# One fused attention and feed-forward kernel: its engine order planned anew, and the first batch's summary rows copied on chip without a transfer

## The chip, the cores and the metric

The kernel runs on one core of a Trainium2 chip. The metric is device time in microseconds (us), the median of three runs. One more execution was profiled; its trace is the source of all rows here.

## The reference

Four batches, eight heads, 768 positions, head size 64. Every query attends to a window of near keys and to 24 summary keys of its sequence; the result goes through a feed-forward block of 512 by 2048.

```python
k_sum = k.reshape(B, H, nb, 32, D).max(axis=3)     # 24 summary keys per head
v_sum = v.reshape(B, H, nb, 32, D).mean(axis=3)    # 24 summary rows of v
scores_l = scale * q @ k.T, kept where |i - j| < 16
scores_s = scale * q @ k_sum.T + log(32)
a = softmax(concat(scores_l, scores_s))
x = a @ concat(v, v_sum)
h = x @ w_in                                       # 3072 x 512 by 512 x 2048
out = (h * erf(softplus(h))) @ w_out
```

## The kernel before

The 3072 rows are worked in six chunks of 512; a chunk has four quads (a quad is one pair of heads in one chunk), so there are 24 quads, numbered in order. For a quad the names are: `scores` (TensorE: mask, near keys, summary keys), `softmax` (VectorE `red`: the row maxima, tile stats; ScalarE `exps`, tile prf; VectorE or ScalarE `norm`), `transp` (TensorE turns the weights, ScalarE copies them to tile ptr), `av` (TensorE: ptr times the value window vw, tile px), `xsplit` (ScalarE or VectorE `high`, VectorE `low`, tile x). The feed-forward block takes the chunks in passes of a quarter of w_in and w_out: `mm1` (tile h), `hout`, activations, `gsplit`, `mm2` (tile ops, lines L1009 and L1013). Float32 operands of the large products are split in a high and a low part, three matmuls for one. Weights arrive packed; `convert` unpacks one unit in three VectorE instructions on tile a, and `split` makes its high part on ScalarE (tile w) and its low part on VectorE.

The last 24 of the 120 rows of each value window of batch 0 are the summary rows. `vsum_first` makes them: six matmul steps on TensorE (tile vs), one copy of the result (tile vsum), and for each of the first four quads one spread of its 24 rows over the eight blocks of the window (tile vwf), which `av` of that quad needs. A spread can be an engine's copy or a transfer on SP's queue.

The order of work is not that of the program text. Every step is handed to a planner, `Plan`, with engines it may run on and a cost in us for each, and with what it reads and writes. `Plan.due` works out from the order of the text when a step would be due; `Plan.order` then goes through time, and at each moment an engine takes, of the steps ready, the one with the lowest key: due time (for TensorE the step's number) plus a correction from the table `TUNE`, which has a row for a step's number: correction, price of an activation table change, which table, and the engine if it is fixed. Every engine's instructions are issued in the planned order, so a step that waits holds up those behind it on its engine; the same goes for SP, which issues the loads. Where the planner sees TensorE idle in the first stage, it puts matmuls on zeros there (`busy`, L1050); seven more stand at the start.

The first steps are numbered: 0 to 7 the loads of keys and queries of quads 0 to 3 (kf, qf in turn), 8 and 9 the values (vt), 10 to 13 the value windows, 14 to 17 the first four weight units; 18 to 27 quad 0's summary keys, scores and softmax (27 its norm), 28 to 35 quad 1's (28 its summary keys, 35 its norm), 36 to 43 quad 2's (43 its norm); 44 to 49 the matmuls of the summary rows, 50 their copy, 51 to 54 the four spreads; 55 to 62 quad 3's (62 its norm); 63 to 72 two weight units; from 73 `transp`, `av`, `xsplit` of quads 0 to 3 with `mm1` between.

```python
key[n] = later + (n if "PE" in o["eng"] else o["due"])
if eng is not None:
    o["eng"] = {eng: o["eng"][eng]}
...
on({"ACT": 0.95, "SP": 0.45} if p else {"DVE": 1.13, "ACT": 0.95}, lambda e, p=p: rows_(e, p), [f"vsum0{p}", f"vwf{p}"], [f"vwg{p}"])
```

Of the kernel before, what the change touches and what calls it, by code (L numbers as in the profile page):

```python
# [58 lines left out]
class Plan:  # L59
# [44 lines left out]
    def order(self, free, window, tune, table):  # L104
# [14 lines left out]
        for o in ops:  # L119
            n = o["n"]  # L120
            later, change[n], which, eng = tune.get(n, (0.0, PEN, 0, None))
            key[n] = later + (n if "PE" in o["eng"] else o["due"])
            if eng is not None:
                o["eng"] = {eng: o["eng"][eng]}
                o["two"] = True
            if o["table"]:
                o["pick"] = o["table"][which]
# [64 lines left out]
def block_attention_mlp(ctx: ExitStack, tc: tile.TileContext, q_t, k_nat, k_win, v_tok, v_nat, v_win, w_in, w_out, out):  # L192
# [16 lines left out]
    def ps(name, tag):  # L209
        return psum.tile([128, 512], F32, name=name, tag=tag)  # L210
# [83 lines left out]
    def first_dma(us, fn, r=(), w=(), **kw):  # L294
        return P.add({"SP": us}, lambda e: fn(), r, w, hold=2.0, land=-1.0, **kw)
# [31 lines left out]
    def load_w(u):  # L327
        kind, g, r = u
        n = raw_slot(u)

        def go():
            rw = raws[u] = slot(n, [128, 2, 512, 2], U32, "rw")
            src = (w_in[2 * g + r] if kind == "i" else w_out[2 * g + r]).bitcast(U32).rearrange("p c (f t) -> p c f t", t=2)
            nc.sync.dma_start(out=rw, in_=src)
        if u in units[:4]:
            first_dma(2.6, go, w=[f"w{n}"])
        else:
            dma(1112, go, w=[f"w{n}"])
# [169 lines left out]
    def load_qk_first(p):  # L508
        st[p] = dict(qb=qfs[:, p], vw=vws[p // 2][:, p % 2])
        first_dma(2.7 if p == 1 else 0.97, lambda: nc.sync.dma_start(out=kfirst[p], in_=k_nat[0, p]), w=[f"kf{p}"])  # L510
        first_dma(0.66, lambda: nc.sync.dma_start(out=qfs[:, p], in_=q_t[0, p]), w=[f"qf{p}"])

    def load_v_first():
        for n in range(2):
            def go(n=n):
                for t in range(3):
                    nc.sync.dma_start(out=vts[n][:, t], in_=v_tok[3 * n + t])
            first_dma(2.1 + 0.15 * n, go, w=[f"vt{n}"])

    def load_vw_first(p):  # L520
        first_dma(1.35, lambda: nc.sync.dma_start(out=st[p]["vw"], in_=v_win[0, p]), w=[f"vwf{p}"])
# [4 lines left out]
    def vsum_first(bank):  # L526
        def go(t):
            if t == 0:
                tiles[bank] = ps("vs", bank)
            nc.tensor.matmul(tiles[bank][0:NK], lhsT=pick[:, 20 - 4 * t:140 - 4 * t], rhs=vts[t // 3][:, t % 3], start=(t == 0), stop=(t == 5))  # L530
        for t in range(6):
            pe(0.87, lambda t=t: go(t), [f"vt{t // 3}"], [bank])
        def summed():
            nc.scalar.copy(vsum[LW:NK], tiles[bank][LW:NK].rearrange("s (p c) -> s p c", p=NP))
        act(0.5, summed, [bank], [f"vsum0{p}" for p in range(NP)])
        def rows_(e, p):
            o, i = st[p]["vw"][LW:NK], vsum[LW:NK, p:p + 1, :].to_broadcast([NS, NB, 128])
            e.dma_start(out=o, in_=i) if e is nc.sync else copy(e, o, i)
        for p in range(NP):
            on({"ACT": 0.95, "SP": 0.45} if p else {"DVE": 1.13, "ACT": 0.95}, lambda e, p=p: rows_(e, p), [f"vsum0{p}", f"vwf{p}"], [f"vwg{p}"])  # L540
# [24 lines left out]
    def load_quad_v(qd):  # L565
        ch, p, seqs = where(qd)
        s = st[qd]

        def go():
            s["vw"] = sb([128, NB, 128], F32, "vw")  # L570
            nc.sync.dma_start(out=s["vw"], in_=v_win[ch, p])
        dma(585, go, w=["vw"])
        for b, js in seqs:
            n = js.stop - js.start
            dma(100 if n == NB else 50, lambda b=b, js=js, n=n: nc.sync.dma_start(out=s["vw"][LW:NK, js], in_=vsum_rows(b, p).to_broadcast([NS, n, 128])),
                [f"vsum{b % 2}{p}"], ["vw"])

    PA = ("pA", "pB")

    def scores(qd, banks=PA):  # L580

        s = st[qd]

        def mask():
            for n in banks:
                tiles[n] = ps(n, n)
            s["sc"] = [tiles[n] for n in banks]
            m0 = mask_at[qd // NP % 3]
            for sc in s["sc"] if qd < MQ else []:

                nc.tensor.matmul(sc[:, 0:NI * NK], lhsT=ident_h, rhs=mask_h[:, m0:m0 + NI], start=True, stop=False, skip_group_check=True)
                nc.tensor.matmul(sc[:, 0:NI * NK].rearrange("q (i c) -> q i c", i=NI)[:, :, LW:NK], lhsT=ones, rhs=cst.rearrange("o (i c) -> o i c", i=NI), start=False, stop=False, skip_group_check=True)

        def keys(parts):
            for j in range(NB):
                for a in range(2):
                    r, o = slice(64 * a, 64 * a + 64), slice(64 * (j % 2), 64 * (j % 2) + 64)
                    for n, rhs in parts(r, j):
                        n += j // 2 * NK
                        nc.tensor.matmul(s["sc"][a][o, n:n + rhs.shape[-1]], lhsT=s["qb"][r, 64 * j:64 * j + 64], rhs=rhs, start=qd >= MQ, stop=True, skip_group_check=True)  # L600

        def near(r, j):

            kn, k0 = kfirst[qd], 64 * j - 16
            return [(0, kn[r, k0:k0 + LW])] if j else [(16, kn[r, 0:LW - 16])]

        def both():
            mask()
            keys(lambda r, j: [(0, s["kw"][r, j])])
        if qd >= NP:  # L610
            pe(0.98 if qd >= MQ else 1.56, both, [f"qb{qd % 2}", f"kw{qd % 2}"] + (["mh"] if qd < MQ else []), banks, small=1)
        else:
            pe(0.58, mask, ["mh"], banks, small=1)
            pe(0.96, lambda: keys(near), [f"qf{qd}", f"kf{qd}"], banks, small=1)
            pe(0.5, lambda: keys(lambda r, j: [(LW, ksum[r, 0, qd])]), [f"qf{qd}", f"ksum0{qd}"], banks, small=1)
# [104 lines left out]
    def av(qd, bank):  # L720
# [3 lines left out]
        def go():  # L724
            xo = s["xo"] = ps("px", bank)
            for j in range(NB):
                o = slice(64 * j, 64 * j + 64)
                for a in range(2):
                    r = slice(64 * a, 64 * a + 64)
                    if qd < DT:  # L730
                        b = 64 * (NI * a + j // 2)
                        nc.tensor.matmul(xo[r, o], lhsT=s["vw"][0:NK, j, r], rhs=s["pt"][0:NK, j % 2, b:b + 64], start=True, stop=True)  # L732
                    else:
                        z = 2 * (j % 2)
                        nc.tensor.matmul(xo[r, o].rearrange("d (a q) -> d a q", a=2), lhsT=s["vw"][0:NK, j, r], rhs=s["pt"][0:NK, z:z + 2, NI * a + j // 2], start=True, stop=True)  # L735
# [572 lines left out]
```

## Time and profile before

| | before |
|---|---|
| median of 3 runs | 600.12 us (599.73 to 600.18) |
| the profiled execution | 599.8 us |
| its span, first to last instruction | 598.0 us, so 1.8 us lie around it |
| mean granted TensorE clock | 0.998 of full speed |
| last matmul ends, last copy ends | 594.05 us, 594.66 us into the span |

PE is TensorE's matmul, PEld its weight load, DVE VectorE, ACT ScalarE, SP the engine whose queue (SPq) issues the loads. A matmul's end in the trace is modelled, and matmuls overlap; the step from one start to the next is shorter than the duration shown.

### The profile page before, as it was taken

The numbers are of one execution on the slowest core, as the hardware profiler recorded it, in microseconds if no ns is written. First come the engines' busy times: TensorE is split into PE (matmuls) and PEld (weight loads), VectorE is DVE, ScalarE is ACT, GpSimd is POOL, SyncE is SP. The second block draws the span as 40 slices with busy tenths as digits, with TensorE's granted clock in tenths as the row PEclk, the third lists the DMA queues.
The fourth block names the chain that finished last, engine by engine and source line by source line (L and its number), as shares of the span: only waits on it lengthen the run. The fifth ranks groups of instructions, "written<-read, shape, count | busy, mean of one in ns | idle before, by whom it ended". The sixth has DMA issues, their size and how long they took to land.

```text
span 598.0 us, 11682 instructions
## 1 busy us (share of the span) xinstructions
PE 590.6 (99%) x4495; PEld 486.1 (81%) x4495; DVE 476.4 (80%) x1001; ACT 424.3 (71%) x824; POOL 4.0 (1%) x30
## 2 busy tenths in 40 slices
PE   8899999999999999999999999999999999999997
PEld 4675666878888889989888888888888888888885
DVE  5999999888999987866989769669778677556553
ACT  6989879989879794674885964846646654852570
POOL 2000000000000000000000000000000000000000
PEclk9999999999999999999999999999999999999999
DMA  8999777668997989899998888787897864774621
GB/s 330 358 418 344 282 253 284 221 247 316 318 344 245 345 323 338 290 351 370 313 376 315 323 310 323 267 302 269 292 304 263 309 226 146 252 243 178 237 72 70
DMA packets 47586, 169.93 MB, mean 284 GB/s; under 512 B 4460, under 2 KB 16940, under 8 KB 34988
## 3 DMA queue, kind: packets, MB, share of 16 engines
q1 hardware_dynamic: 47388, 169.07, 78.1%
q8 instruction: 35, 0.57, 0.4%
q14 instruction: 19, 0.16, 0.1%
q10 hardware_dynamic: 144, 0.13, 0.1%
HBM read 135.66 MB, written 31.46 MB: 279 GB/s over the span
## 4 chain that ended last, share of the span: by engine, by line
PE 96%; ACT 1%; DVE 1%; issue 0%
PE ops L1013 41%; PE h L839 15%; PE ha L891 12%; PE hb L885 7%; PE ops L1009 5%; PE hb L891 4%; PE hb L882 4%; PE pA L600 3%; PE px L735 3%; PE px L732 1%; DVE stats L639 1%; PE pA L687 1%; PE idle L1050 1%; ACT prf L647 0%; PE pB L600 0%; ACT ptr L692 0%
## 5 line engine op out<-in xcount | busy, mean ns | idle before, releaser
L1013 PE MATMUL ops<-w,gh 128*128 128x512 f32 x704 | 230.1, 393 | 0.0
L1013 PEld LDWEIGHTS ops<-w,gh 128*128 128x128 f32 x704 | 132.3, 188 | 27.8 <-issue 0.9
L1013 PE MATMUL ops<-w,gl 128*128 128x512 f32 x352 | 137.5, 391 | 0.0
L1264 ACT ACT_TABLE_LOAD x98 | 125.7, 1283 | 1.7
L839 PE MATMUL h<-x,w 128*128 128x512 f32 x384 | 97.0, 402 | 0.0
L298 ACT COPY hc<-hb 128x256 f32<-128x256 f32 x65 | 23.9, 373 | 102.9 <-PE hb L882 57.0
L839 PEld LDWEIGHTS h<-x,w 128*128 128x128 f32 x384 | 71.1, 188 | 18.5 <-issue 3.6
L1013 PEld LDWEIGHTS ops<-w,gl 128*128 128x128 f32 x352 | 66.2, 188 | 11.8
L989 DVE TENSOR_TENSOR hc<-wt,hc 128x1024 f32<-128x1024 f32 x44 | 53.0, 1219 | 10.7 <-ACT wt L977 10.7
L647 ACT ACTIVATE prx<-prx,stats 128x120 f32<-128x120 f32 x160 | 61.0, 384 | 0.2
L996 DVE TENSOR_TENSOR gl<-hc,gh 128x1024 fp32r<-128x1024 f32 x44 | 53.6, 1220 | 1.0 <-ACT gh L298 0.2
L930 DVE TENSOR_TENSOR hc<-hb,hc 128x256 f32<-128x256 f32 x96 | 38.7, 418 | 15.8 <-ACT hc L298 14.6
L977 ACT ACTIVATE wt<-wt 128x1024 f32<-128x1024 f32 x48 | 50.1, 1058 | 0.4
L965 ACT ACTIVATE wt<-hc 128x1024 f32<-128x1024 f32 x32 | 33.0, 1055 | 8.2 <-DVE hc L930 8.0
L298 DVE CAST gh<-hc 128x1024 fp32r<-128x1024 f32 x37 | 25.5, 690 | 10.6 <-PE ops L1013 9.5
L885 PE MATMUL hb<-w,ws 128*128 128x512 f32 x96 | 30.2, 396 | 0.0
L647 ACT ACTIVATION_READ_ACCUMULATOR prx<-prx,stats 128x1 f32 x160 | 30.0, 187 | 0.0
L1009 PE MATMUL ops<-a32s,gw 128*128 128x512 f32 x64 | 29.6, 597 | 0.0
L633 DVE CUSTOM_DVE_ANT_0 prx<-pA,mask_sb 128x120 f32<-128x120 f32 x64 | 14.2, 278 | 17.7 <-PE pB L600 17.4
L298 DVE COPY hc<-hb 128x256 f32<-128x256 f32 x31 | 13.0, 418 | 18.0 <-PE hb L882 13.8
L891 PE MATMUL ha<-w,ws 128*128 128x256 f32 x192 | 27.2, 283 | 0.0
L891 PE MATMUL ha<-x,w 128*128 128x256 f32 x192 | 27.1, 282 | 0.0
(172 smaller groups left out, 959.8 us busy)
## 6 DMA issues: line engine op xcount, KB each, us to landing
w<-dr SPq DMA_DIRECT2D x36, 1024.0 KB
ws<-ds SPq DMA_DIRECT2D x30, 1024.0 KB
vw<-v_win SPq DMA_DIRECT2D x20, 512.0 KB
kw<-k_win SPq DMA_DIRECT2D x20, 480.0 KB
rw<-w_in SPq DMA_DIRECT2D x8, 1024.0 KB
rw<-w_out SPq DMA_DIRECT2D x8, 1024.0 KB
dr<-w SPq DMA_DIRECT2D x8, 1024.0 KB
dt<-ot SPq DMA_DIRECT2D x16, 512.0 KB
```

The lines of the kernel that those rows point to most:

```text
L298: e.copy(o, i) if e is nc.scalar else e.tensor_copy(o, i)
L647: nc.scalar.activation(s["pr"][:, j], s["pr"][:, j] if qd >= MQ else s["sc"][j // NI][:, i * NK:(i + 1) * NK], AF.Exp, scale=-1.0 if qd >= ...
L839: nc.tensor.matmul(hs[k, f][:, 0:T], lhsT=w[m], rhs=xt[ch, cc][:, x], start=(cc == 0 and n == 0), stop=(cc == 3 and n == 2))
L885: nc.tensor.matmul(full, lhsT=w[0], rhs=y, start=first and c == 0, stop=c == 1, skip_group_check=True)
L891: nc.tensor.matmul(half, lhsT=w[m], rhs=y[:, l], start=first and c == 0 and i == 0, stop=c == 1 and i == 2, skip_group_check=True)
L930: on({"DVE": 0.43}, lambda e: e.tensor_tensor(hc[k, n][:, m, z], bank(n, "b")[:, R], hc[k, n][:, m, z], op=ALU.add), [pair_banks(n)[1]], [ ...
L977: act(0.96, lambda n=n: nc.scalar.activation(wt[k, n], wt[k, n], AF.Erf, scale=-1.0 if k < SOFT else 1.0), [s], [s], table=("sig",), after ...
L989: e.tensor_tensor(hc[k, n], wt.pop((k, n)), hc[k, n], op=ALU.mult)
L996: e.tensor_tensor(gs[k, n][1], hc.pop((k, n)), f32(gs[k, n][0]), op=ALU.subtract)
L1009: nc.tensor.matmul(os_[ch, t], lhsT=x[0][:, i % 2, t * 128:(t + 1) * 128], rhs=w32["o", g, i // 2][:, i % 2], start=first, stop=last)
L1013: nc.tensor.matmul(os_[ch, t], lhsT=x[y][:, i % 2, t * 128:(t + 1) * 128], rhs=w[m], start=first and n == 0, stop=last and n == 2)
L1264: nc.scalar.preload_act_table_set(sets[o["load"]])
```

## The change

Three things are edited. The correction table `TUNE` is replaced as a whole: 1303 rows for 1114, 8 of them as before, with numbers up to 2101 in both. The planner's costs of the first loads and of a few first-stage steps are set to other values, and the first eight loads get keys of their own that put them in the order 0, 1, 3, 2, 8, 4, 5, 9. The spread of the summary rows may run on ScalarE or VectorE only; the new table puts all four on ScalarE, where before three were there and quad 2's was a transfer on SP. The copy of the summary rows (50) may now be VectorE's too, and the table keeps it on ScalarE. `OWN` and `ASKED` are empty, so their branches issue nothing; the number of steps is the same. In the table the rows are shown broken over lines, those of the steps that the text speaks of.

```diff
-TUNE = {0: (-400.0, 1.5, 0, None), 1: (-300.0, 1.5, 0, None), 2: (-100.0, 1.5, 0, None), 3: (-200.0, 1.5, 0, None),
...
-27: (392.5856, 1.5, 0, None), 35: (42.72401, 1.5, 0, None), 43: (39.54326, 1.5, 0, None),
-51: (-22.99868, 1.5, 0, 'ACT'), 52: (-1.271128, 1.5, 0, 'ACT'), 53: (0, 1.5, 0, 'SP'), 54: (-212.8407, 1.5, 0, 'ACT'),
-62: (-0.1662937, 1.5, 0, 'ACT'),
...
+TUNE = {0: (-25.14396, 1.5, 0, None), 2: (0.2021052, 1.5, 0, None),
...
+27: (31.6296, 1.5, 0, None), 28: (-7.221647, 1.5, 0, None), 35: (3.818883, 1.5, 0, 'DVE'), 43: (13.99603, 1.5, 0, 'DVE'),
+50: (86.021, 1.5, 0, 'ACT'), 51: (50.85707, 1.5, 0, 'ACT'), 52: (23.98324, 1.5, 0, 'ACT'), 53: (0.01018608, 1.5, 0, 'ACT'), 54: (0.09698313, 1.5, 0, 'ACT'),
...
-            key[n] = later + (n if "PE" in o["eng"] else o["due"])
+            key[n] = later + (n if "PE" in o["eng"] else o.get("first", o["due"]))
-        return P.add({"SP": us}, lambda e: fn(), r, w, hold=2.0, land=-1.0, **kw)
+        return P.add({"SP": us}, lambda e: fn(), r, w, hold=2.0, land=-0.9, **kw)
-            first_dma(2.6, go, w=[f"w{n}"])
+            first_dma(2.5, go, w=[f"w{n}"])
-        first_dma(2.7 if p == 1 else 0.97, lambda: nc.sync.dma_start(out=kfirst[p], in_=k_nat[0, p]), w=[f"kf{p}"])
-        first_dma(0.66, lambda: nc.sync.dma_start(out=qfs[:, p], in_=q_t[0, p]), w=[f"qf{p}"])
+        first_dma((1.05, 1.0, 1.0, 1.0)[p], lambda: nc.sync.dma_start(out=kfirst[p], in_=k_nat[0, p]), w=[f"kf{p}"])
+        first_dma((0.65, 1.4, 0.65, 0.65)[p], lambda: nc.sync.dma_start(out=qfs[:, p], in_=q_t[0, p]), w=[f"qf{p}"])
-            first_dma(2.1 + 0.15 * n, go, w=[f"vt{n}"])
+            first_dma(2.0 + 0.85 * n, go, w=[f"vt{n}"])
-        first_dma(1.35, lambda: nc.sync.dma_start(out=st[p]["vw"], in_=v_win[0, p]), w=[f"vwf{p}"])
+        first_dma(1.28, lambda: nc.sync.dma_start(out=st[p]["vw"], in_=v_win[0, p]), w=[f"vwf{p}"])
-        act(0.5, summed, [bank], [f"vsum0{p}" for p in range(NP)])
+        on({"ACT": 0.55, "DVE": 0.6}, lambda e: copy(e, vsum[LW:NK], tiles[bank][LW:NK].rearrange("s (p c) -> s p c", p=NP)), [bank], [f"vsum0{p}" for p in range(NP)])
-            on({"ACT": 0.95, "SP": 0.45} if p else {"DVE": 1.13, "ACT": 0.95}, lambda e, p=p: rows_(e, p), [f"vsum0{p}", f"vwf{p}"], [f"vwg{p}"])
+            if p in OWN:
+                P.last[f"vwg{p}"] = ()
+            elif p in ASKED:
...
+            else:
+                on(VWG, lambda e, p=p: rows_(e, p), [f"vsum0{p}", f"vwf{p}"], [f"vwg{p}"])
+    OWN, ASKED = (), ()
+    VWG = {"ACT": 0.95, "DVE": 1.13}
-            pe(0.96, lambda: keys(near), [f"qf{qd}", f"kf{qd}"], banks, small=1)
-            pe(0.5, lambda: keys(lambda r, j: [(LW, ksum[r, 0, qd])]), [f"qf{qd}", f"ksum0{qd}"], banks, small=1)
+            pe(0.92, lambda: keys(near), [f"qf{qd}", f"kf{qd}"], banks, small=1)
+            pe(0.57, lambda: keys(lambda r, j: [(LW, ksum[r, 0, qd])]), [f"qf{qd}", f"ksum0{qd}"], banks, small=1)
...
+    for n, p in enumerate((0, 1, 3, 2, 8, 4, 5, 9)):
+        P.ops[p]["first"] = n - 1e6
```

## Rows read from the trace of the kernel before

**Rows 1.** The page: busy us of each engine, share of the span, instructions.

```profile
PE 590.6 (99%) x4495; PEld 486.1 (81%) x4495; DVE 476.4 (80%) x1001; ACT 424.3 (71%) x824; POOL 4.0 (1%) x30
```

**Rows 2.** Busy time by stage: window, its length, then each engine, clock, DMA share, GB/s.

```profile
6.67:15.00 8.33, 7.67 (x145) 4.42 (x144) 7.36 (x17) 5.74 (x33) 0.34 (x3) 1.00 1.04 405
15.00:24.17 9.17, 7.45 (x142) 4.61 (x141) 9.03 (x14) 9.03 (x25) 0.00 (x0) 1.00 1.03 415
...
26.00:45.00 19.00, 19.00 (x151) 14.94 (x150) 18.86 (x23) 17.03 (x34) 0.00 (x0) 1.00 1.00 397
45.00:60.00 15.00, 15.00 (x75) 8.49 (x74) 15.00 (x31) 14.87 (x32) 0.00 (x0) 1.00 0.92 347
60.00:90.00 30.00, 30.00 (x217) 19.40 (x215) 29.83 (x66) 24.22 (x43) 0.00 (x0) 1.00 0.74 267
...
150.00:590.00 440.00, 440.00 (x3172) 380.70 (x3171) 338.53 (x725) 289.48 (x520) 0.00 (x0) 1.00 0.78 280
```

**Rows 3.** Waits of TensorE's matmuls, whole run: total us, times, longest.

```profile
PE pA L687 <- ACT ptr L692: 1.3, 1, 1.3
PE idle L1050 <- DVE zeros L217: 1.1, 1, 1.1
PE h L600 <- DVE ksum L524: 0.7, 1, 0.7
PE px L732 <- ACT vwf L298: 0.4, 1, 0.4
```

**Rows 4.** Chain of waits, 0 to 34 us: start, us on the chain, work.

```profile
8.28 0.86 DVE ksum L524
...
12.45 1.07 DVE prf L657
13.52 1.14 DVE stats L639 x2
...
14.95 2.85 ACT prf L647 x16
```

**Rows 5.** Timeline of TensorE: start, us, instructions; in brackets the idle time before.

```profile
9.19 0.66 PE L600 MATMUL h<-ksum,qf 64*64 64x24 f32 x32 [0.66 <-DVE ksum L524]
...
12.51 0.66 PE L600 MATMUL o<-ksum,qf 64*64 64x24 f32 x32
...
21.58 1.25 PE L1050 MATMUL idle<-zeros 128*128 128x512 bf16 x5
24.17 0.24 PE L687 MATMUL pA<-ident,prf 64*120 64x64 f32 x1 [1.34 <-ACT ptr L692]
```

**Rows 6.** Timeline of ScalarE, 17 to 24.2 us.

```profile
18.79 0.58 ACT L534 COPY vsum<-vs 24x512 f32<-24x512 f32 x1
19.40 1.04 ACT L298 COPY vwf<-vsum 24x1024 f32<-24x1024 f32 x1
20.46 1.04 ACT L298 CAST w<-a 128x1024 fp32r<-128x1024 f32 x1
21.53 1.04 ACT L298 COPY vwf<-vsum 24x1024 f32<-24x1024 f32 x1
22.60 0.58 ACT L298 CAST x<-px 128x512 fp32r<-128x512 f32 x1
23.08 0.59 ACT L692 COPY ptr<-pA 120x512 f32<-120x512 f32 x1
```

**Rows 7.** Waits of SP's queue: total us, times, longest.

```profile
SPq L538 <- DMA vwf<-v_win: 10.1, 1, 10.1
```

**Rows 8.** Busy time from 24 to 27 us, columns as in Rows 2.

```profile
24.00:27.00 3.00, 2.83 (x53) 2.55 (x54) 2.93 (x5) 2.98 (x18) 0.00 (x0) 1.00 0.60 158
```

**Rows 9.** Chain of waits, whole run: shares by line, and its longest piece.

```profile
by line: PE ops L1013 40.8%; PE h L839 15.1%; PE ha L891 11.5%; PE hb L885 7.4%; PE ops L1009 4.7%; PE hb L891 3.8%; PE hb L882 3.7%; PE pA L600 3.1%; PE px L735 2.9%; PE px L732 1.3%; DVE stats L639 0.6%; PE pA L687 0.6%; PE idle L1050 0.6
...
574.29 19.76 PE ops L1013 x87
```

**Rows 10.** Timeline of ScalarE: the norm of quad 3.

```profile
29.36 2.40 ACT L660 ACTIVATE prf<-prf,stats 128x120 f32<-128x120 f32 x8
```

More of the change, by code (lines that the diff above doesn't have):

```diff
@@ L532, in vsum_first, with rows_ @@
             pe(0.87, lambda t=t: go(t), [f"vt{t // 3}"], [bank])
-        def summed():
-            nc.scalar.copy(vsum[LW:NK], tiles[bank][LW:NK].rearrange("s (p c) -> s p c", p=NP))
-        act(0.5, summed, [bank], [f"vsum0{p}" for p in range(NP)])
-        def rows_(e, p):
+        on({"ACT": 0.55, "DVE": 0.6}, lambda e: copy(e, vsum[LW:NK], tiles[bank][LW:NK].rearrange("s (p c) -> s p c", p=NP)), [bank], [f"vsum0{p}" for p in range(NP)])
+        def rows_(e, p, ask=False):
             o, i = st[p]["vw"][LW:NK], vsum[LW:NK, p:p + 1, :].to_broadcast([NS, NB, 128])
-            e.dma_start(out=o, in_=i) if e is nc.sync else copy(e, o, i)
+            e.dma_start(out=o, in_=i) if ask or e is nc.sync else copy(e, o, i)
         for p in range(NP):
-            on({"ACT": 0.95, "SP": 0.45} if p else {"DVE": 1.13, "ACT": 0.95}, lambda e, p=p: rows_(e, p), [f"vsum0{p}", f"vwf{p}"], [f"vwg{p}"])
+            if p in OWN:
+                P.last[f"vwg{p}"] = ()
+            elif p in ASKED:
+                act(0.4, lambda p=p: rows_(nc.scalar, p, True), [f"vsum0{p}", f"vwf{p}"], [f"vwq{p}"])
+                P.add({"POOL": 2.2}, lambda e: None, [f"vwq{p}"], [f"vwg{p}"])
+            else:
+                on(VWG, lambda e, p=p: rows_(e, p), [f"vsum0{p}", f"vwf{p}"], [f"vwg{p}"])
     def load_quad(qd):
@@ L725, in go @@
             xo = s["xo"] = ps("px", bank)
+            for a in range(2 if qd in OWN else 0):
+                r = slice(64 * a, 64 * a + 64)
+                rhs = s["pt"][LW:NK, :, 256 * a:256 * a + 256].rearrange("k x (n q) -> k n x q", n=NI)
+                nc.tensor.matmul(xo[r].rearrange("d (n x q) -> d n x q", n=NI, x=2), lhsT=vsum[LW:NK, qd, r], rhs=rhs, start=True, stop=False, skip_group_check=True)
             for j in range(NB):
@@ L731, in go @@
                         b = 64 * (NI * a + j // 2)
-                        nc.tensor.matmul(xo[r, o], lhsT=s["vw"][0:NK, j, r], rhs=s["pt"][0:NK, j % 2, b:b + 64], start=True, stop=True)
+                        nk = LW if qd in OWN else NK
+                        nc.tensor.matmul(xo[r, o], lhsT=s["vw"][0:nk, j, r], rhs=s["pt"][0:nk, j % 2, b:b + 64], start=qd not in OWN, stop=True, skip_group_check=qd in OWN)
                     else:
@@ L735, in go @@
                         nc.tensor.matmul(xo[r, o].rearrange("d (a q) -> d a q", a=2), lhsT=s["vw"][0:NK, j, r], rhs=s["pt"][0:NK, z:z + 2, NI * a + j // 2], start=True, stop=True)
-        pe(1.085, go, ["pt", "vw"] if qd >= NP else ["pt", f"vwf{qd}", f"vwg{qd}"], [bank], small=1)
+        pe(2.1 if qd in OWN else 1.15 if qd < NP else 1.085, go, ["pt", "vw"] if qd >= NP else ["pt", f"vwf{qd}", f"vsum0{qd}" if qd in OWN else f"vwg{qd}"], [bank], small=1)
     xt = {}
```

2 lines of the change are left out of this document (1 added, 1 removed).

## The prediction

> **What bounds the kernel now.** I read the page first. TensorE shows 99% busy [rows 1]; VectorE with 80% and ScalarE with 71% have room over the whole span, and that average says nothing of one stage. So next came the busy times by stage. The reader is to see two different kernels in them. From 26 us on, TensorE is busy for the whole of each stage, up to 590 us [rows 2]; no later matmul is in the list of TensorE's waits, which has four entries in all, and all four lie before 24.2 us [rows 3]. Before 26 us it is idle for 0.66 of 8.33 us and then for 1.72 of 9.17 us. An order of the engines can therefore take time away in two places: in this first stage, where the waits are, and in the matmul stream behind it, where a pause could hide only below the modelled ends.
>
> In the first stage the timeline of TensorE shows where the time goes: 0.66 us before the summary keys of quad 1 at 9.19 us, 0.4 us before the first `av` [rows 3], and from 21.58 us, when five matmuls on zeros start, to 24.17 us, when the next real one starts: 24.17 - 21.58 = 2.59 us [rows 5]. Together that is 3.65 us, the most that the first stage can give as long as it does the same matmuls.
>
> The three are not independent. The chain of waits runs through them, and it runs on VectorE and ScalarE: summary keys of quad 1 on VectorE at 8.28 us, their matmuls, the maxima of quads 1 and 2, the exponentials of quad 2 on ScalarE at 14.95 us [rows 4], then ScalarE without a break until TensorE can go on [rows 6]. From 15 us both engines are 98% busy (9.03 of 9.17 us) [rows 2]. What shortens this chain moves the whole matmul stream; what only fills a pause beside it does not.
>
> **The change part by part.** I sum along that chain, against the profiled execution's 599.8 us.
>
> First, the summary keys of quad 1 (step 28, whose correction is now -7.2, ahead of its due time). Their VectorE instruction begins at 8.28 us [rows 4], after both halves of quad 0's maxima, and TensorE waits 0.66 us for its end [rows 5]. If it goes in front of the second half, TensorE has no wait; the second half, on which quad 0's later exponentials hang, is then late by that instruction, 0.86 us, but those exponentials end well before quad 2's begin at 14.95 us, which hides it. Gain 0.66 us; bounds 0 (the order stays) and 0.66. I take 0.66.
>
> Second, quad 0's norm. It stands on VectorE at 12.45 us for 1.07 us, and quad 2's maxima only start at 13.52 us [rows 4], while the matmuls that they need end at 12.51 + 0.66 = 13.17 us [rows 5]. The norm is not needed before quad 0's transposes. With the maxima first, the chain is 13.52 - 13.17 = 0.35 us shorter, and the norm moves behind them. Bounds 0 and 0.35. Both corrections are small now (27 has 31.6, 43 has 14.0), so that the key does not exclude it; I take 0.35.
>
> Third, ScalarE from 18.79 to 24.17 us. It copies the summary rows (0.58 us), spreads quad 0's (1.04), rounds a weight unit (1.04), spreads quad 1's (1.04), rounds x (0.58), and only then copies the transposed weights of quad 1 [rows 6], for which TensorE waits [rows 3]. Of these, quad 1's spread is not needed by the copy behind it: it is needed one step later, by quad 1's `av`, and TensorE has quad 2's transposes to do in between. In the new table quads 0 and 1 have late keys for their spreads (corrections 50.9 and 24.0) and early ones for the rounding of x. One copy out from in front of the wait is worth its 1.04 us. Bounds: 0, if another instruction takes its place, and 2.59 us, the whole gap. I take 1.04, the price of one instruction.
>
> Fourth, quad 2's spread. It leaves SP's queue and comes to ScalarE: one copy, 1.04 us by the rows of the other two [rows 6]. On the chain it would cost 1.04 us. It is wanted by quad 2's `av` only, after the stream has started; from 26 to 45 us ScalarE is idle for 19.00 - 17.03 = 1.97 us [rows 2], which holds it. Besides, quad 3's norm ran on ScalarE for 2.40 us [rows 10] and is no longer fixed there; on VectorE the same work took 1.07 us [rows 4]. Taken at 0, bounds 0 and +1.04.
>
> Fifth, SP. The transfer made SP's queue stand for 10.1 us, until quad 2's value window had landed [rows 7]; behind it waited the fourth weight unit, quad 3's value window and all loads of the next quads. When it was gone the DMA engines had run dry: 158 GB/s from 24 to 27 us [rows 8] against 415 before [rows 2]. That is 3.0 x (415 - 158) = 0.77 MB, or 1.9 us at 415 GB/s, by which the later loads can now land sooner. I cost it at nothing, for what hides it is that nobody waited for them: VectorE is idle for 0.14 us from 26 to 45 us, and not at all to 60 us [rows 2]. The loads keep their places behind the ones that the first stage needs, so I see no loss either. The new costs of loads and matmuls only enter the plan. Step 50 stays on ScalarE, and `OWN` and `ASKED` issue nothing: 0 each.
>
> Sixth, everything after 26 us. The same instructions come in another order. The chain gives L1013 40.8% of 598.0 us for 1056 matmuls, 231.0 ns each, and L839 15.1% for 384, 235.2 ns each; the closing run of 87 needs 19.76 us, 227.1 ns each [rows 9]. The difference is 4.1 + 3.1 = 7.2 us, which is what order can touch in these two lines, changes between small and large matmuls included. I find no reason for a sign, and take 0, with a third of it, 2.4 us, either way.
>
> Sum: -0.66 - 0.35 - 1.04 = -2.05 us, so 597.75 us for the profiled execution. The median of the runs was 0.32 us above that execution, so **598.1 us** is forecast.
>
> [...]
>
> **The rivals.** *The gap only moves (24%).* ScalarE is full from 15 us, and it gets a fourth spread. If that copy, +1.04 us, lands before the stream's start, it eats the third gain, and only 0.66 + 0.35 is left, of which VectorE, 98% busy too, may keep part: 599.1 to 600.1 us. For it speaks that both engines are saturated; against it, that quad 2's `av` is not the first.
>
> *Pauses below the modelled ends close as well (8%).* [...] A third of 7.2 us on top of the gain gives 598.1 - 2.4 = 595.7 us. Against it: nothing in the rows after 26 us shows TensorE waiting.
>
> *VectorE comes late and it gets slower (18%).* Between 26 and 90 us VectorE is idle for 0.14 + 0.00 + 0.17 = 0.31 us in 64 us [rows 2]. TensorE is never held up by it there, which needs every VectorE result to come just in time. A stream that starts 2.05 us sooner asks for them sooner. If a pass needs a split weight or an x while the planner has put VectorE passes of some 1.07 us in front, TensorE waits that long, in a stage that had no wait. It decides from 2.05 + 1.2 = 3.25 us, three such passes; four cost 4.28 us, which gives 598.1 + 4.28 = 602.4 us. Against it: VectorE does unpacking there for later passes, which can be put off.
>
> *The change does not do what it says:* excluded for SP, as all four spreads are fixed on ScalarE; for the rest it is the first rival.
>
> **How the numbers follow.** The gain of about 2 us has 50%, with a range of its own from 597.1 us (1 us more of the 2.59 us gap) to 598.9 us (the third gain at a quarter). The first rival has 24%, the second 8%, the third 18%. The measurement tells about 0.2% from no change, 1.2 us. So faster has 50 + 8 = 58%, the same 24%, slower 18%. The range from 596.4 to 601.6 us holds the forecast, the first rival and half of the others; outside lie about 4% below and 11% above.
>
> **What would show it.** Right: no wait before quad 1's summary-key matmuls; quad 2's maxima within 0.1 us of their matmuls' end; the copies of quad 1's ptr before quad 1's spread or right after x; the first L839 matmul some 2 us sooner than before; four spreads on ScalarE, none on SPq, and no drop of DMA traffic at 24 us; TensorE still 100% busy from 26 to 590 us. Wrong: the first L839 matmul less than 1 us sooner, new entries in TensorE's list of waits between 26 and 150 us with VectorE as releaser, or a number of L1013 steps far from 231 ns. What would make the forecast wrong is above all the part that I could not see, the order of 2,000 later steps.

## The result: 603.63 us, slower, and a stop in the middle of the first `av`

| | before | after |
|---|---|---|
| median | 599.96 us (5 runs, 599.73 to 600.18) | 603.63 us (5 runs, 602.41 to 604.34) |
| ratio | | 1.0056, 95% interval 1.0042 to 1.007 |
| span of the profiled execution | 598.0 us | 601.7 us |
| first `mm1` matmul | 25.96 us | 29.18 us |
| from there to the end of the span | 572.0 us | 572.5 us |

The forecast was 598.1 us, the range ended at 601.6 us. Of the 3.7 us between the spans 3.2 are lost before the first `mm1` matmul and 0.5 behind it, so the first stage is where to read on. Lines of the kernel have moved: L600 is now L606, L639 L645, L647 L653, L657 L663, L660 L666, L687 L693, L692 L698, L732 L743, L839 L850, L1013 L1024, L1050 L1061.

The page of the changed kernel, in answer to [rows 1], says almost nothing of it:

```profile
PE 592.0 (98%) x4495; PEld 486.9 (81%) x4495; DVE 480.3 (80%) x1008; ACT 405.8 (67%) x802; POOL 4.0 (1%) x30
```

The busy times by stage, columns as in [rows 2], do:

```profile
6.67:15.00 8.33, 7.70 (x159) 4.60 (x157) 7.35 (x17) 6.31 (x34) 0.34 (x3) 1.00 1.03 405
15.00:24.17 9.17, 6.07 (x114) 3.69 (x112) 8.80 (x13) 7.03 (x22) 0.00 (x0) 1.00 1.04 414
24.00:27.00 3.00, 2.63 (x22) 1.26 (x24) 1.75 (x4) 2.07 (x6) 0.00 (x0) 0.72 1.01 422
26.00:45.00 19.00, 19.00 (x186) 15.22 (x185) 18.14 (x23) 14.92 (x34) 0.00 (x0) 0.93 0.85 337
150.00:590.00 440.00, 439.29 (x3169) 379.98 (x3168) 342.96 (x734) 274.20 (x520) 0.00 (x0) 1.00 0.79 280
```

From 15 to 24.17 us TensorE is busy for 6.07 us, where it was 7.45. ScalarE, which was full there, has 2 us of rest: it is not what holds TensorE. The waits of TensorE, as in [rows 3], name the piece:

```profile
PE px L743 <- issue: 2.9, 1, 2.9
PE idle L1061 <- DVE zeros L217: 1.1, 1, 1.1
PE h L850 <- ACT hc L298: 0.7, 1, 0.7
PE h L606 <- DMA kf<-k_nat: 0.6, 1, 0.6
PE h L606 <- DVE ksum L524: 0.2, 1, 0.2
```

"issue" means that the engine waited for nothing that the profile shows: no semaphore, no landing, no other engine. The timeline of TensorE shows the place; it answers to [rows 5]:

```profile
20.57 0.91 PE L743 MATMUL px<-ptr,vwf 120*64 120x64 f32 x23 [0.17 <-ACT vwf L298]
24.36 0.50 PE L743 MATMUL px<-ptr,vwf 120*64 120x64 f32 x9 [2.88 <-issue]
24.80 1.83 PE L1061 MATMUL idle<-zeros 128*128 128x512 bf16 x5
...
27.60 1.65 PE L743 MATMUL px<-ptr,vwf 120*64 120x64 f32 x32
```

And the same view of the kernel before:

```profile
20.49 1.15 PE L732 MATMUL px<-ptr,vwf 120*64 120x64 f32 x32 [0.38 <-ACT vwf L298]
...
24.88 1.15 PE L732 MATMUL px<-ptr,vwf 120*64 120x64 f32 x32
```

The 32 matmuls of the first `av` have the same operands and no wait between them. After 23 of them TensorE stands for 2.88 us. A wait for data would stand ahead of the first. What is left is that TensorE lacks its instructions, an inference that the experiments on their count, below, put to the test. The DMA view has a queue of the kind instruction, q8. The page of this kernel counts 35 packets on it, 0.57 MB, so 16 KB each:

```profile
q8 instruction: 35, 0.57, 0.4%
```

TensorE has 4495 matmuls and as many weight loads [rows 1], 9109 recorded instructions with its semaphore instructions; 9109 / 35 makes one packet per 260. The same view from the start to 21.6 us shows two such packets before (at 10.53 and 16.91 us; a third follows at 24.04):

```profile
q8 instruction: 2, 0.03, 0.6%
```

After, it shows one:

```profile
q8 instruction: 1, 0.02, 0.3%
```

The second one starts at 21.66 us here instead of 16.91, and TensorE goes on 2.7 us after that start. Counting recorded TensorE instructions, it had done 705 when it stopped; e6, below, stops at 449, which is 256 less. Steps of 256 back from 705 lead to 449 and 193, and from 193 to the end there are 35 such boundaries, as many as packets, in this trace and in that of before. In both, every packet from the fourth on starts within 4.6 us of the time at which TensorE passes the boundary of the same number. That the packets of q8 are TensorE's is read from these counts; the trace does not name the engine.

The 256 instructions from one such boundary to the next are called a block below. The second packet starts 7.8 us after TensorE has passed instruction 449 (13.89 us), where before it starts 1.8 us after (15.16 us).

The stop has a second price. In stretches of one microsecond (columns as in [rows 2]) the granted clock falls from 1.00 to 0.50 after TensorE has stood:

```profile
24.00:25.00 1.00, 0.64 (x10) 0.48 (x11) 0.30 (x1) 0.10 (x1) 0.00 (x0) 1.00 1.01 422
25.00:26.00 1.00, 1.00 (x4) 0.35 (x3) 0.48 (x1) 1.00 (x3) 0.00 (x0) 0.67 1.04 434
26.00:27.00 1.00, 1.00 (x10) 0.44 (x10) 0.96 (x3) 0.97 (x4) 0.00 (x0) 0.50 0.99 410
27.00:28.00 1.00, 1.00 (x22) 0.88 (x20) 1.00 (x1) 1.00 (x7) 0.00 (x0) 0.50 1.06 442
28.00:29.00 1.00, 1.00 (x28) 1.00 (x26) 0.97 (x2) 1.00 (x7) 0.00 (x0) 0.63 0.99 410
```

The second `av` falls in it, 1.65 us instead of 1.15, and quad 2's transposes ahead of it, 1.03 us (26.57 to 27.60) instead of 0.71 (24.17 to 24.88): 0.8 us in all. Up to the first `mm1` matmul the sum is this: the first `av` starts 0.1 us later and takes 4.29 us instead of 1.15; the slower clock costs 0.8 us; the pause from the end of that `av` to the transposes is 0.8 us shorter, since ScalarE does quad 1's spread while TensorE stands. That makes the 3.2 us. The other half microsecond, behind the first `mm1` matmul, fits the one new wait there, 0.7 us of an `mm1` matmul for a copy on ScalarE (the wait list), which is also what TensorE lacks of the 440 us from 150 to 590 us (the stages).

### The profile page after: what moved, and what is told of

The parts are those of the page before. It is cut to its first block, busy times and chain, and to the rows that moved or that the text cites. A ratio compares the mean times of both kernels' runs of the same rounds, so it can differ in the third digit from the quotient of the medians.

```text
span 601.7 us, 11678 instructions
## 1 busy us (share of the span) xinstructions
PE 592.0 (98%) x4495; PEld 486.9 (81%) x4495; DVE 480.3 (80%) x1008; ACT 405.8 (67%) x802; POOL 4.0 (1%) x30
## 4 chain that ended last, share of the span: by engine, by line
PE 90%; DMA 5%; ACT 3%; issue 1%; SPq 1%; ACTq 0%
PE ops L1024 39%; PE h L850 12%; PE ha L902 11%; PE hb L896 7%; PE ops L1020 4%; PE hb L902 4%; PE hb L893 4%; PE px L746 3%; PE pA L606 3%; PE px L743 2%; DMA vwf<-v_win 2%; DMA dr<-w 1%; DMA vw<-v_win 1%; DMA kf<-k_nat 1%; ACT L1277 1%
## 5 line engine op out<-in xcount | busy, mean ns | idle before, releaser
L1024 PE MATMUL ops<-w,gh 128*128 128x512 f32 x704 | 227.8, 393 | 0.0
L1024 PEld LDWEIGHTS ops<-w,gh 128*128 128x128 f32 x704 | 132.3, 188 | 28.3 <-issue 1.3
L1024 PE MATMUL ops<-w,gl 128*128 128x512 f32 x352 | 137.4, 390 | 0.0
L298 ACT COPY hc<-hb 128x256 f32<-128x256 f32 x70 | 25.9, 372 | 116.3 <-PE hb L893 58.8
L850 PE MATMUL h<-x,w 128*128 128x512 f32 x384 | 93.1, 396 | 0.9 <-ACT hc L298 0.7
L850 PEld LDWEIGHTS h<-x,w 128*128 128x128 f32 x384 | 71.2, 188 | 18.7 <-issue 1.4
L1024 PEld LDWEIGHTS ops<-w,gl 128*128 128x128 f32 x352 | 66.2, 188 | 12.1
L653 ACT ACTIVATE prx<-prx,stats 128x120 f32<-128x120 f32 x160 | 61.0, 384 | 0.2
L298 DVE CAST gh<-hc 128x1024 fp32r<-128x1024 f32 x41 | 28.3, 690 | 14.0 <-PE ops L1024 13.5
L653 ACT ACTIVATION_READ_ACCUMULATOR prx<-prx,stats 128x1 f32 x160 | 30.0, 187 | 0.0
L639 DVE CUSTOM_DVE_ANT_0 prx<-pA,mask_sb 128x120 f32<-128x120 f32 x64 | 14.2, 279 | 17.8 <-PE pB L606 17.5
L902 PE MATMUL ha<-x,ws 128*128 128x256 f32 x192 | 26.9, 282 | 0.0
```

The source lines that it names most:

```text
L298: e.copy(o, i) if e is nc.scalar else e.tensor_copy(o, i)
L653: nc.scalar.activation(s["pr"][:, j], s["pr"][:, j] if qd >= MQ else s["sc"][j // NI][:, i * NK:(i + 1) * NK], AF.Exp, scale=-1.0 if qd >= ...
L850: nc.tensor.matmul(hs[k, f][:, 0:T], lhsT=w[m], rhs=xt[ch, cc][:, x], start=(cc == 0 and n == 0), stop=(cc == 3 and n == 2))
L902: nc.tensor.matmul(half, lhsT=w[m], rhs=y[:, l], start=first and c == 0 and i == 0, stop=c == 1 and i == 2, skip_group_check=True)
L1024: nc.tensor.matmul(os_[ch, t], lhsT=x[y][:, i % 2, t * 128:(t + 1) * 128], rhs=w[m], start=first and n == 0, stop=last and n == 2)
```

## The experiments

In all of them the finished plan is edited: `move(steps, to)` puts steps behind step `to` (or before it), which changes the order on their engines; `on` is the engine. "Small matmuls" are products of zeros into the bank of the idle matmuls, 64 columns each, read by nobody; each is two TensorE instructions. Ratios are to the kernel before on the same chip, with 95% intervals. In the six sets of runs, 16 of 140 executions of the kernel before took 602 us or more, against medians of 599.96 to 600.53 us (one of 3329.93 us is left out, and one of e17 of 833.2 us).

### Is it the loads, or SP that no longer stands?

**e1**: the new order, quad 2's spread as a transfer again.

```diff
+    by[53]["on"] = "SP"
+    move([53], 16)
```

> The new order, with quad 2's spread put back on SP's queue behind the third weight unit, so that SP stands again until quad 2's value window has landed; nothing else moves. Theory A (TensorE's own instructions come late because SP goes on issuing loads after 14 us while the DMA engines are full): the 2.88 us pause inside the first av is gone, the clock stays at its upper level, and the time falls by 2.9 us and some 0.7 us of low clock to about 600.0 us. Theory B (the pause belongs to the new order of TensorE's instructions, whatever SP does): the pause stays and the time is 603.6 us. Theory C (the loss is ScalarE's, from the fourth spread): 603.6 - 1.04 = 602.6 us with the pause unchanged.

SP stood again for 7.6 us, though only from 17.0 us (13.9 before), and DMA fell to 320 GB/s from 24 to 27 us (422 without). 603.44 us, ratio 1.004 (1.0024 to 1.0055); the stop was there with 2.89 us. Letting SP stand from there does not take it away.

**e2**: the old order, quad 2's spread on ScalarE.

```diff
+    by[53]["on"] = "ACT"
+    move([53], 71, before=True)
```

> The old order, with quad 2's spread taken from SP's queue to ScalarE, just ahead of the rounding of the second weight unit (about 28 us), so that SP never stands; nothing else moves. Theory A: a pause of 2 to 3 us of the kind that waits for nothing shown appears in the old order too, near the same count of TensorE's instructions, at about 21 us, and the time rises to 602 to 603.5 us. Theory B: no such pause; 600 to 601 us, the 1.04 us copy at most.

601.49 us, ratio 1.0012 (0.9998 to 1.0026), no stop in the profile. The loads go on, 412 GB/s from 24 to 27 us, and the second packet starts at 17.83 us: with e1, SP's freedom is not the cause. What the copy on ScalarE costs ahead of step 71 is not clear of the noise.

**e5**: the new order, the second weight unit's load behind two value windows.

```diff
+    move([15], 13)
```

> The new order, with the second weight unit's load (1 MB) put behind the value windows of quads 2 and 3 on SP's queue. The runs so far show that the 2.9 us pause comes when the next block of TensorE's instructions is fetched late, at the same count of instructions in either order. Theory D (the fetch stands behind that one large load): the fetch comes through by 18.5 us, no pause in the first av, 600.0 to 601.0 us. Theory E (what decides is when TensorE gets to the end of the block before; SP's order of loads does not matter): the pause stays, 603.0 to 604.0 us.

603.13 us, ratio 1.005 (1.0037 to 1.0062). The loss stays in all five executions (602.40 to 604.28 us), so the place of this load does not take it away. In the profiled one the second packet started at 20.78 us, the stop was 1.32 us and the first `mm1` matmul came at 26.99 us, 2.2 us sooner than without the edit; but from there to the end it took 574.2 us instead of 572.5, at a mean granted clock of 0.949, where the other four have 0.994 to 0.997. So its total says nothing of the shorter stop.

### Is it one of the moved steps?

**e4**: the old order with the third term of the sum alone, quad 1's spread behind the copies of quad 1's ptr.

```diff
+    move([52], 79)
```

> The old order, with one thing moved on ScalarE: quad 1's spread goes behind the copies of quad 1's transposed weights instead of in front of the rounding of x. This is the third term of the forecast alone. If that term was right, quad 2's transposes start about 1.04 us sooner (23.1 us instead of 24.17) and the time falls by up to 1 us to 599.0. Rival: VectorE's norm of quad 2 ends at 24.03 us and holds them just as well, and quad 1's spread is then late for its av; 0 to +1 us, 600 to 601.

600.43 us, ratio 1.0004 (0.9988 to 1.0021): the gain of the third term does not come. Its profiled execution, 603.0 us, has the stop. Timeline of TensorE:

```profile
20.90 0.97 PE L732 MATMUL px<-ptr,vwf 120*64 120x64 f32 x25 [0.52 <-ACT vwf L298]
24.36 0.65 PE L732 MATMUL px<-ptr,vwf 120*64 120x64 f32 x7 [2.49 <-issue]
```

The old order can stop in the same way, with SP's queue as it was, again after instruction 705, which in this order is the 25th pair of the `av`. What the change did was to make a rare stop the rule.

The mean granted clock, which is on record for every execution, bears this out. Of the twenty profiled ones, the eight with a stop in the first `av` have 0.997 or less, the twelve without 0.998 or more. By that sign 17 of 135 executions of the kernel before had the stop, all 16 at 602 us or more among them, but all 5 of the changed kernel and all 12 of e1, and three of 12 of e2. It parts the executions of a single kernel too: of e14 below, three have it, at 602.75 to 603.26 us, and nine have not, at 599.79 to 600.31 us; of e12, six have it, at 602.47 to 605.29 us, and one has not, at 600.07 us. It is a sign and no proof: e16 has three times around 602.2 us at a full clock.

**e7**: the new order with the transposes of quads 0 and 1 and the copies of quad 0's back where they were.

```diff
+    move([56], 47)
+    move([73], 56)
+    move([57], 78, before=True)
+    move([74], 41)
```

> The new order, with quad 0's transposes and their copies put back where the old order has them: on TensorE behind quad 3's mask, on ScalarE behind quad 2's exponentials. Theory E (the early transposes bring TensorE to the end of its block sooner, 13.9 us for 15.2 us, and so the next fetch is late): the pause comes in few runs, as in the old order (6 of 29 at 601.2 us or more): median 600.0 to 600.8 us. Theory D (SP's loads decide): unchanged, 603 to 604 us.

601.35 us, ratio 1.0015 (1.0006 to 1.0024), no stop, second packet at 17.77 us. **e8** does the counterpart, the old order with quad 0's transposes early.

```diff
+    move([73], 47, before=True)
+    move([74], 41, before=True)
```

> The old order, with quad 0's transposes put in front of the fourth matmul of the summary rows and their copies in front of quad 2's exponentials, as the new order has them. The counterpart of the run before. Theory E: the pause comes in most runs, 602.5 to 603.5 us median. Theory D: as before, 600.3 us, with the pause in one run of five.

600.37 us, ratio 0.9998 (0.9983 to 1.0013), no stop, packet at 18.36 us. Neither of the two moves the transposes alone. `busy` fills the pauses that it reckons from the planned times, so ahead of the first `av` e7 has ten matmuls on zeros where the new order has one, and e8 four where the old one has none: 18 and 8 instructions more. The theory that the early place brings the stop found no support in e8; that the late place takes it away in e7 is not shown, since the count changed with it. Nor is it shown why e7 is 0.15% slower than before without a stop in its profile.

### Is it the count of instructions?

**e3** and **e6** (one kernel, a single execution and a timed set): the new order, six small matmuls ahead of step 30, quad 1's near keys.

```diff
+    for _ in range(6):
+        nc.tensor.matmul(idle[:, 0:64], lhsT=zeros[:, 0:128], rhs=zeros[:, 0:64], start=True, stop=True)
```

> The new order, with six small matmuls on zeros (twelve instructions) put in front of quad 1's near keys, where TensorE waits 0.63 us for a load anyway. They compute nothing that is used. Theory A: the pause comes at the same count of instructions, so six matmuls sooner in the first av, after 17 of its 32 instead of 23; the time stays within 602.4 to 604.4 us. Rival (the pause belongs to a wait of the av's own, for data): it stays after 23.

> The kernel with six more small matmuls on zeros once more, timed. The single run before had the pause one block of instructions sooner, 1.5 us long, and none in the first av. If that is what the shift does and no chance: median 600.5 to 601.5 us, in most runs below 602. If it was chance: 603 to 604 us.

600.9 us, and in the set 600.32 us, ratio 0.9998 (0.9982 to 1.0013). Twelve instructions that compute nothing give back the whole loss. The waits of e6's TensorE:

```profile
PE pA L693 <- DVE prf L663: 1.5, 1, 1.5
PE vs L530 <- issue: 1.2, 1, 1.2
```

A stop of 1.2 us is now one block sooner (at instruction 449, which is 705 less 256), at 14.35 us, where it is partly covered. **e9** puts one long matmul, two instructions, in the same place; **e12** puts the six small ones directly ahead of the first `av`; **e15** takes four, eight instructions, at e6's place.

> The new order with one matmul of 512 columns on zeros (two TensorE instructions, about 0.25 us) at the place where six small ones (twelve instructions, about 0.3 us) took the loss away. If the number of instructions decides where TensorE must wait for its next block, two are too few to move it far: the pause of about 2.9 us stays inside the first av, now after 22 of its 32 matmuls instead of 23, and the time stays at 603 to 604 us. If the small delay of the stream was what helped, the pause is gone and the time is about 600.3 us.

> The new order with the six small matmuls directly ahead of the first av. By the count, the pause comes after 17 of the first av's 32 matmuls instead of 23, in the same block, which is asked for no sooner than in the new order: it stays 2 to 3 us, and the time 603 to 604 us. If any twelve instructions ahead of the pause help, it is gone and the time is about 600.3 us.

> The new order with four small matmuls (eight instructions) ahead of quad 1's summary-row step instead of six (twelve). The earlier boundary then falls directly behind quad 2's summary-key matmuls, at about 12.8 us, where TensorE has to stop for the block: no pause in the first av, 600.0 to 600.5 us, and a pause of about 1 us at the boundary before. If twelve were needed, 603 to 604 us as without them.

e9: 603.18 us, ratio 1.0051 (1.0039 to 1.0063). e12: 604.12 us, 1.0056 (1.0035 to 1.0076). e15: 600.89 us, 1.0006 (0.9989 to 1.0023). Timeline of TensorE in e9:

```profile
20.44 0.91 PE L743 MATMUL px<-ptr,vwf 120*64 120x64 f32 x22
24.32 0.56 PE L743 MATMUL px<-ptr,vwf 120*64 120x64 f32 x10 [2.96 <-issue]
```

In e12:

```profile
20.37 0.74 PE L743 MATMUL px<-ptr,vwf 120*64 120x64 f32 x17
24.05 1.12 PE L743 MATMUL px<-ptr,vwf 120*64 120x64 f32 x15 [2.95 <-issue]
```

In e15:

```profile
20.31 0.80 PE L743 MATMUL px<-ptr,vwf 120*64 120x64 f32 x19 [0.16 <-ACT vwf L298]
22.56 0.74 PE L743 MATMUL px<-ptr,vwf 120*64 120x64 f32 x13 [1.45 <-issue]
```

Two instructions more and the stop comes after 22 pairs instead of 23; eight, 19; twelve, 17. It sits at an instruction's number and at no time and no step. (For e15 no stop in the `av` was expected; it came, at half the length.) e12 has the same count ahead of the `av` as e6, and the full loss: the added work is not what helps, but where it stands: in e6 the stop is at the boundary before.

### What makes the block late?

The theory then: the block is late if TensorE runs over the boundary before it (instruction 449) without a stop and soon after the first packet. **e11** puts e6's six small matmuls into the old order, **e13** three at the same place, **e14** three directly ahead of the first `av`.

> The old order with the same six small matmuls on zeros ahead of the same step. If the shift by itself is worth something (a later boundary is simply better), the old order gains too, or at least loses its occasional times of 602 us and more: 599.5 to 600.2 us, none over 601.2. If the shift only moves where the boundary falls, the old order, which mostly had its block in time, gains nothing and may lose: 600.3 to 602 us.

> The old order with three small matmuls on zeros (six TensorE instructions) ahead of the step where six of them (twelve instructions) cost it nothing. Theory: the block that the first av needs comes late when TensorE runs over the boundary before it (256 instructions earlier) without a stop, within some 3 us of the first fetch of the stage; it comes in time when TensorE gets there 3.8 us or more after that fetch, or has to stop there. Six instructions put the old order's earlier boundary into the matmuls of the summary rows at about 14.4 us, 3.0 us after the fetch: the pause of 2.5 to 3 us comes into most runs, now after 22 of the first av's matmuls, and the median is 602.5 to 604 us. Rival: only the number of instructions ahead of the av counts, and twelve or none were harmless in this order: 600.2 to 600.6 us.

> The old order with the same three small matmuls, but directly ahead of the first av: the same number of instructions ahead of the boundary inside it, while the earlier boundary stays where the old order has it, at about 15.1 us. If the earlier boundary decides, this is as the old order: 600.2 to 600.6 us and a pause in a minority of runs. If the boundary inside the av decides, it is as the kernel with the three matmuls further ahead, whatever that is.

e11: 600.39 us, ratio 1.0001 (0.9993 to 1.001). e13: 600.08 us, 1.0002 (0.999 to 1.0013). e14: 600.06 us, 1.0005 (0.9987 to 1.0024). None had the stop in its profile; e13 should have. By the clock of all executions, too, one of 12 had it in e13 (603.05 us), three of 12 in e14, none of 11 in e11. The theory fell. From the traces, in us:

```
kernel               instr. 449 passed     second packet         stop at instr. 705
before, e2           15.16, 15.48          16.91, 17.83          none
e7, e8, e14          15.21, 15.34, 15.22   17.77, 18.36, 17.22   none
e3, e6, e11, e17     stopped to 13.9-14.4  18.31, 18.24, 18.21, 17.75   none
e10, e18             stopped to 13.1-13.5  17.38, 17.18          none
e13                  14.42                 17.42                 none
after, e1            13.89, 13.65          21.66, 21.84          2.88, 2.89
e4, e5               14.86, 14.75          21.82, 20.78          2.49, 1.32
e9, e12              14.26, 14.06          21.63, 21.62          2.96, 2.95
e15, e16             13.74, 14.23          19.95, 20.45          1.45, 1.61
```

What stays is a pattern with an exception: where TensorE passes the boundary at 15 us or later, or has to stop there (0.1 to 1.5 us), the next packet starts at 18.36 us or sooner; where it passes sooner without a stop, at 19.95 us or later, but not in e13. The eight stops in the `av` end 2.36 to 2.73 us after the start of this packet (24.36 - 21.66 = 2.70 us in the changed kernel), which starts at 19.95 us at the soonest and at 21.84 at the latest: so the reading here is that TensorE stands for this packet. The time at which a fetch is asked for is in no trace here, and so why it is late stays open.

### Was there something to gain in the gap?

**e10**: e6 with quad 2's norm on VectorE ahead of quad 3's maxima. **e16** and **e17**: that and quad 1's spread behind the copies, with four and with six small matmuls. **e18**: the edits of e17 in the old order.

```diff
+    move([43], 59, before=True)
+    move([52], 79)
```

> The new order with the six small matmuls, and quad 2's norm on VectorE ahead of quad 3's maxima. In the shifted run TensorE waited 1.5 us for that norm before quad 2's transposes. If VectorE's order is what bounds the gap there, the wait falls by up to 1.2 us and the time to 599.1 to 599.6 us, under both kernels. If ScalarE or a landing bounds it just as well (the transposed weights of quad 1 are copied until 25.1 us there), the gain is under 0.3 us and the time stays at 600.0 to 600.5 us. If quad 3's maxima, now 1.07 us later, hold the next quad, it is slower, 601 us.

> The new order with four small matmuls, quad 2's norm on VectorE ahead of quad 3's maxima, and quad 1's spread on ScalarE behind the copies of quad 1's transposed weights. Either alone was worth nothing, since the other held the same gap. If the two together set its end, TensorE starts quad 2's transposes about 1.1 us sooner, the first mm1 matmul is at about 25.5 us, and the median is 598.8 to 599.6 us, under both kernels. If a landing or quad 3 takes their place, 600.0 to 600.6 us.

> The two edits of the gap together (quad 2's norm ahead of quad 3's maxima, quad 1's spread behind the copies of quad 1's transposed weights) in the new order with six small matmuls, with which the first av had no pause. If the two together set the end of the gap, the first mm1 matmul is at 25.3 to 25.8 us and the median is 598.9 to 599.7 us, under both kernels. If something else holds the gap as well, 600.0 to 600.6 us. If the pause comes back with the edits, 601 to 602.5 us, and the number of instructions alone was not what kept it away.

> The same two edits and the six small matmuls in the old order. If the gap is all that the first stage had to give, the first mm1 matmul is about 1.1 to 1.5 us sooner than in the old order with the six matmuls alone (26.99 us), and the median is 599.0 to 599.5 us. If quad 1's spread, now behind the copies, holds quad 1's av as long, 600.0 to 600.5 us.

e10: 600.46 us, ratio 1.0001 (0.9987 to 1.0016). e16: 601.81 us, 1.0019 (1.0 to 1.0038), with a stop of 1.61 us in the `av`, as e15 has. e17: 600.55 us, 0.9994 (0.9978 to 1.001); e18: 600.22 us, 0.9994 (0.9986 to 1.0002). Waits of TensorE in e10, where VectorE's norm is gone from e6's list and the copies stand in its place:

```profile
PE pA L693 <- ACT ptr L698: 0.9, 1, 0.9
PE vs L530 <- issue: 0.4, 1, 0.4
```

and the timeline of e17's TensorE, where the copies are out of the way too and the spread is awaited one step later:

```profile
25.28 1.15 PE L743 MATMUL px<-ptr,vwf 120*64 120x64 f32 x32 [0.65 <-ACT vwf L298]
26.36 3.74 PE L850 MATMUL h<-x,w 128*128 128x512 f32 x15
```

Three things hold the gap, within about a microsecond of one another: VectorE's norm of quad 2, ScalarE's copies, and the spread. e17's first `mm1` matmul is 0.8 us sooner than e6's (27.18 us), and 0.4 us later than before's. No version here is shown to be faster than the kernel before.

## Why the prediction was wrong, step by step

**The step that failed** is in its first part: "Together that is 3.65 us, the most that the first stage can give", and the sum that follows. It counts as TensorE's possible waits only those for other engines and landings. A term for the delivery of TensorE's own instructions was missing, and it measured +2.88 us, with 0.8 us of slower clock behind it. The trace of before had the packets on q8, three by 25 us, and nobody waited for them; that another order could stand for them could not be seen from the waits, since there were none. e6 shows the size: without the stop in the `av` the new order stands at 0.9998 of the old (0.9982 to 1.0013), so the stop is the loss, within 0.2%. The forecast missed by 5.5 us because this came on top and the gain of 2.05 us did not come, as the terms show.

**First term, 0.66 us forecast.** The order came as described: quad 1's summary keys stand between the halves of quad 0's maxima. Timeline of VectorE after:

```profile
7.45 0.95 DVE L524 TENSOR_REDUCE ksum<-kf 128x24 f32<-128x768 f32 x1 [0.22 <-DMA kf<-k_nat]
8.32 0.65 DVE L645 TENSOR_REDUCE stats<-pB 128x4 f32<-128x480 f32 x1
...
12.32 1.16 DVE L663 TENSOR_TENSOR prf<-prf,stats 128x960 f32<-128x960 f32 x1
13.40 1.22 DVE L645 TENSOR_REDUCE stats<-o 128x4 f32<-128x480 f32 x2
```

The wait ahead of their matmuls is gone, as forecast. Timeline of TensorE after:

```profile
7.56 0.89 PE L606 MATMUL h<-kf,qf 64*64 64x80 f32 x32 [0.63 <-DMA kf<-k_nat]
...
8.98 0.66 PE L606 MATMUL h<-ksum,qf 64*64 64x24 f32 x32
```

The 0.2 us of the wait list are quad 3's, at 19.42 us. But TensorE now waits 0.63 us for the landing of quad 1's keys, which was hidden. The summary-key matmuls start at 8.98 us instead of 9.19, so 0.2 us of the 0.66 are left here, and nothing of them at the first `av` (20.57 us against 20.49).

**Second term, 0.35 us forecast.** It did not happen: quad 0's norm, at 12.32 us, still stands ahead of quad 2's maxima, which start at 13.40 us instead of 13.52 [rows 4]. That bound of 0, "the order stays", was the right one.

**Third term, 1.04 us forecast.** Not in the new order either. Timeline of ScalarE, in answer to [rows 6]:

```profile
18.35 0.58 ACT L298 COPY vsum<-vs 24x512 f32<-24x512 f32 x1
19.48 1.04 ACT L298 COPY vwf<-vsum 24x1024 f32<-24x1024 f32 x1 [0.55 <-DMA vwf<-v_win]
20.54 1.05 ACT L298 CAST w<-a 128x1024 fp32r<-128x1024 f32 x1
21.61 1.04 ACT L298 COPY vwf<-vsum 24x1024 f32<-24x1024 f32 x1
24.91 0.59 ACT L298 CAST x<-px 128x512 fp32r<-128x512 f32 x1 [2.25 <-PE px L743]
...
30.89 2.00 ACT L298 COPY vwf<-vsum 24x1024 f32<-24x1024 f32 x2
```

The same five stand in the same order; quad 1's spread is still ahead of x and the copies. Reading an order out of corrections failed here. And done by hand (e4, e10, e17) the term gives no time, since the norm, the copies and the spread hold the gap in turn. The trace of before had the norm already: VectorE ends quad 2's at 22.88 + 1.15 = 24.03 us, 0.14 us ahead of the transposes that need it, so that taking a copy out could not give 1.04 us. Timeline of VectorE before:

```profile
22.88 1.15 DVE L657 TENSOR_TENSOR prf<-prf,stats 128x960 f32<-128x960 f32 x1
```

What the copy of the summary rows won, 18.79 - 18.35 = 0.44 us, went into a wait of 0.55 us for quad 0's value window: 19.48 us against 19.40, and the first `av` at 20.57 against 20.49.

**Fourth and fifth, 0 and 0.** Right. The two spreads are at 30.89 us, behind the stream's start. DMA ran on with 422 GB/s from 24 to 27 us where it had 158 [rows 8], nobody gained by it, and e1 and e2 show that it is not the cause of the loss.

**Sixth, 0 with 2.4 us either way.** Right: from the first `mm1` matmul to the end it was 572.0 us before, 572.5 after, 572.0 in e6 and 571.7 in e10. The 2000 later steps, which the prediction feared most, moved half a microsecond. The first `mm1` matmul, named as the sign that would tell, came 3.2 us later instead of 2 us sooner.

**The rivals.** No run shows the 2.4 us that pauses closing below the modelled ends were to give: behind the first `mm1` matmul the new order took 0.5 us more. VectorE late behind 26 us did not come: from 30 to 150 us TensorE waits once, 0.2 us. "The gap only moves", 599.1 to 600.1 us, is close to what the new order gives once the stop is taken away (600.32 us, with 1.2 us of a stop still in it). Slower was forecast by the wrong mechanism; what came was no rival of the prediction.

## What to carry to other kernels

A wait that the profile puts down to issue, in the middle of equal matmuls that have all their operands, was here, by the counts, a wait for instructions (2.88 us, after 23 of 32): look for the instruction packets in the DMA view, count instructions to the place, and shift it with a few empty ones before believing in any cause among the data. Where the granted clock of every execution is on record, it can hint at how often such a stop comes even where no trace was taken; here it was 0.997 or less with the stop in the `av` and 0.998 or more without, in twenty profiled executions. Where an order is made new for a stage that loads as this one does, 414 GB/s, set the stage's gains against such a stop, 1.32 to 2.96 us here, that no wait of the old trace announces. And a gap that three things hold within a microsecond is not worth the price of the one that is named.

## What the runs showed of the hardware that was not expected

Packets of 16 KB, TensorE's instructions by their count, came beside the loads, which ran at 414 GB/s from 15 to 24.17 us, and the second one started at 16.91 us in the old order and at 21.66 us in the new; in all eight stops in the `av` TensorE went on 2.36 to 2.73 us after the start of this packet. Twelve instructions more or fewer ahead of one step were worth 3.3 us of 600 (603.63 against 600.32 us, e6, from two sets). After a stop of 2.88 us the granted clock was 0.50 from 26 to 28 us, although it had been 1.00 from 15 to 24.17 us.
